# Two pairs of heads in one stretch of attention matmuls, in an attention and SwiGLU kernel on Trainium2

## The chip, the cores and the metric

The kernel runs on one core of one Trainium2 chip. The metric is device time in microseconds (us) of one execution; lower is better. The core's engines are TensorE (PE in the profile; PEld is its weight load), VectorE (DVE), ScalarE (ACT), GpSimd (POOL) and SyncE (SP, which here only issues transfers). They run side by side, each through its own list of instructions in order, and wait for each other by semaphores. Matmuls write PSUM, which has eight banks; everything else lies in SBUF or in device memory.

## The reference

```python
def rmsnorm(x, g):
    return x / np.sqrt(np.mean(x * x, axis=-1, keepdims=True) + 1e-06) * g
q_n, k_n = rmsnorm(q, g_q), rmsnorm(k, g_k)        # q, k, v: (8, 12, 448, 64), float32
scores = np.matmul(q_n, k_n.transpose(0, 1, 3, 2)) / np.sqrt(64)
attn = np.exp(scores - scores.max(-1, keepdims=True))
attn = attn / (attn.sum(-1, keepdims=True) + 1e-09)
x = np.matmul(attn, v)                             # -> rows of (8 * 448, 12 * 64)
xn = rmsnorm(x, rms_g)                             # over 768 columns
g = xn @ w_gate                                    # 768 x 1536
out = (g / (1 + np.exp(-g)) * (xn @ w_val)) @ w_out
```

There are eight sequences of 448 tokens with 12 heads of 64, then a feed-forward net (FFN) over all 3584 tokens, all in float32.

## The kernel before, in words

**Attention** goes by pairs of heads, two heads side by side on the 128 partitions: pairs 0 to 47, six to a sequence, so pair g is place g mod 6 of sequence g // 6. Scores are made transposed, in seven parts of 64 keys by 448 queries a head. `step(g, i)` does three things: the two score matmuls of part i of pair g into a bank of the scores pool (`ps_s`, four banks, tag "s"), the two matmuls of part i of the pair before (`weighted(g - 1, i)`: values by exponentials, into the tile `av`), and the exponentials of the new scores on ACT into a tile `e` (11 buffers). Each of these matmuls uses a quarter of the array, 64 by 64, and the four of a step run side by side. So one call of seven steps makes the scores of pair g and the weighted values of pair g - 1. I call such a run of attention matmuls between FFN matmuls an **excursion**.

The softmax's denominators are made off TensorE: `later_sums(g, n)` has POOL add the seven `e` tiles of a pair into `es` (six adds, lines 904 and 909). At every even pair, `totals(g - 1)` sums two pairs' `es` over the keys with a few small matmuls into `den` (scores pool), ACT copies them, DVE inverts them, and `weigh` multiplies: x = av * rd. ACT then squares x, and POOL adds the squares to `ss`, for the norm ahead of the FFN. After an odd pair the kernel only puts `av` aside (`hold`, one ACT copy), and weighs it at the next `totals`. `av` lies in `ps_m`, a pool of one bank, which the transposes of q and k (tile `tr`) use too.

**The FFN** of a sequence is worked off while the next sequence's attention runs. For the first sequence it is plain matmuls. From the second on, gate and value are 4 groups of 15 products in a scheme with fewer multiplications (`three`; a **product** is four matmuls with 128x128 weights and 224 columns, line 1419), and the out projection has 7 products, or two levels of 7 (`out_quads`, line 1778). Sums of blocks are made by DVE (lines 989, 1610, 1638 and others). The weights are converted once from float64 by DVE, ACT and POOL, while the first sequence's FFN runs; sums of weight blocks are made by DVE during the second (`derive`, lines 1311 to 1346) and third (`derive_q`, lines 1377 to 1380), written to device memory (`kept`, `kept_o`, `kept_q`), and read again by SP into a ring of slots (`w`) for each sequence. A slot is asked for again when TensorE has used it.

**The order** is written out by hand. `pe(fn)` emits a piece of TensorE's work and counts one step; `after(n, fn)` emits something n steps later; `light(fn)` puts small DVE work on a list that is emitted between FFN items. The main loop goes over the pairs. The turn of pair g (places 1 to 5) is: its excursion, then a third of the turn's FFN items (`fill`), the norms and squares of the pairs ahead, the transposes of q and then k of pair g + 1 with another `fill` between them, and a last `fill`. So between two excursions lies the FFN work of one turn, and excursions and FFN alternate from pair 8 to the end. A `fill(hold=True)` leaves one weight conversion of its last item to be emitted within the next excursion.

Until its weights are all made the FFN also depends on the place of an excursion: `derive_q` is tried once within each excursion, and within `fill` only more than four steps after the last excursion's end (`st["block"]`).

`yard` is one SBUF tile in which places for q, k, v, their norms and other small things are cut out by hand (`spot`).

Of the kernel before, what the change touches and what calls it, by code (L numbers as in the profile page):

```python
# [335 lines left out]
def safe_scores(  # L336
# [42 lines left out]
    def after(n, fn):  # L379
        due.append((now["t"] + n, fn))  # L380
# [41 lines left out]
    AT_QK = PER_B  # L422
    AT_V = AT_QK + 3 * PAIR
    AT_OTHER = AT_V + 3 * THIRD
    AT_RS = AT_V
    AT_V1 = AT_RS + 7 * NB
    yard = slots.tile([128, AT_OTHER + PER_B], F32, name="yard")

    def spot(at, n):
        return yard[:, at:at + n]  # L430

    def turned(g):

        return g >= TURNED * NPAIR
# [30 lines left out]
    def squares_turned(g):  # L465

        qk, n = st["qk", g], 2 * NB
        ms = st["ms", g] = spot(AT_RS, 2 * n).rearrange("p (a n) -> p a n", a=2)
        rs = st["rs", g] = spot(AT_RS + (4 + g % 2) * NB + g % 2 * NB // 2, NB + NB // 2)
        def reduce(i, sq):  # L470
            nc.vector.tensor_reduce(out=ms[:, 0, i * NB:(i + 1) * NB], in_=blocks(sq), axis=AX_X, op=ALU.add)
            if i == 1:
                after(1, other)
                after(2, total)
                after(2, root)

        for i in range(2):
            sq = new_sq()
            nc.scalar.activation(sq, qk[:, i], ACT.Square)
            light(lambda i=i, sq=sq: reduce(i, sq))  # L480
        every, first, second = slice(0, NB), slice(NB, NB + NB // 2), slice(NB + NB // 2, n)
        both = slice(0, NB + NB // 2)

        def other():
            for at in (0, 64):
                nc.scalar.copy(ms[at:at + 32, 1, both], ms[at + 32:at + 64, 0, both])
                for to, of in ((every, every), (first, second)):
                    nc.scalar.copy(ms[at + 32:at + 64, 1, to], ms[at:at + 32, 0, of])
# [326 lines left out]
    def weighted(g, i):  # L815

        b, hp = divmod(g, NPAIR)
        if i == 0:
            st["av", g] = ps_m.tile([128, 512], F32, name="av", tag="m")
        for j in range(2):  # L820
            r = across(j)
            vt = st["v", g][r, i] if turned(g) else st["vr", b][r, hp] if i == PARTS - 1 else st["v", g][r, i // NK, i % NK]
            nc.tensor.matmul(st["av", g][own(j), 0:S], lhsT=vt, rhs=st["e", g, i][r], start=i == 0, stop=i == PARTS - 1,  # L823
                             skip_group_check=True)

    def step(g, i):
# [2 lines left out]
        weighted(g - 1, i)  # L829
        if ps is not None:  # L830
            exps(g, i, ps)

    AT_ALIKE = AT_OTHER
    AT_FEW = AT_ALIKE + 128

    def late(g):

# [24 lines left out]
    def totals_folded(g):  # L862

        which = (g - 1, g)
        den = ps_s.tile([128, 512], F32, name="den", tag="s")[:, 0:2 * NB]
        for j in range(2):
            nc.tensor.matmul(den[own(j)], lhsT=alike()[across(j), own(j)], rhs=some_few(0, 2)[across(j)], start=True, stop=True)
        few = some_few(2, 2)
        nc.vector.reciprocal(few, den)
        for i in which:  # L870
            rd = st["rd", i] = tmp.tile([128, S], F32, name="rd", tag="rd", bufs=2)
            nc.vector.transpose(out=blocks(rd), in_=few[:, i % 2 * NB:(i % 2 + 1) * NB].unsqueeze(2).to_broadcast([128, NB, 32]))
            if i < g:
                weigh(i, 3, 4)

    def totals(g):

        if folded(g):
            totals_folded(g)
            return  # L880
        which = (g, g - 1) if g > NPAIR + 1 else (g,)
        den = {i: ps_s.tile([128, 512], F32, name="den", tag="s") for i in which[::-1]}
        for i in which:
            es = st.pop(("es", i))
            for j in range(2):
                to = j if i == g else 1 - j
                nc.tensor.matmul(den[i][own(to), 0:S], lhsT=ones[across(j)], rhs=es[across(j)], start=True, stop=True)
        for i in which[::-1]:
            rd = st["rd", i] = tmp.tile([128, S], F32, name="rd", tag="rd", bufs=2)
            if i == g:  # L890
                nc.scalar.copy(rd, den[i][:, 0:S])
            else:
                for j in range(2):
                    nc.scalar.copy(rd[own(j)], den[i][across(j), 0:S])
        for i in which[::-1]:
            invert(st["rd", i], st["rd", i])
            if i < g:
                weigh(i, 3, 4)

    def later_sums(g, n):  # L900

        def first():
            st["es", g] = tmp.tile([128, S], F32, name="es", tag="es", bufs=2)
            nc.gpsimd.tensor_tensor(st["es", g], st["e", g, 0], st["e", g, 1], ALU.add)  # L904
            more(2)

        def more(*parts):
            for i in parts:
                nc.gpsimd.tensor_tensor(st["es", g], st["es", g], st["e", g, i], ALU.add)  # L909

        after(n, first)
        after(n + 2, lambda: more(3, 4))
        after(n + 3, lambda: more(5, 6))
        if folded(g):
            after(n + 8, lambda: light(lambda: fold(g)))

# [1143 lines left out]
            convert()  # L2060


    at_once(squares(0, 0))
    warm(15)
    reduce, root, scale = norm_rests(0, 0, 2)
# [16 lines left out]
    for g in range(NG + 1):  # L2082
# [51 lines left out]
        if g == NPAIR + 1:  # L2134
# [8 lines left out]
            later_sums(g, 2)  # L2143
            begin(0, 15)
        else:
            hurry_light()
            sums_due = g % 2 == 0
            pe(lambda: (totals(g - 1) if sums_due else None, step(g, 0)))
            if st.pop("held", None):
                convert()  # L2150
            pe(lambda: [step(g, i) for i in (1, 2)])
            derive_q()
            pe(lambda: [step(g, i) for i in (3, 4)])
            pe(lambda: ([step(g, i) for i in (5, 6)], weigh(g - 1, 2) if sums_due else hold(g - 1)))
            if g < NG:
                later_sums(g, 11 if g == 3 * NPAIR else 2)
        st["block"] = now["t"]
        for n in (1, 2):
            if turned(g + n) == (n == 1):
                after(2, lambda g=g + n: load_v(g))  # L2160
        if hp:
            fill()
            norm_k(g + 1, 0)
            if not turned(g + 2):
# [74 lines left out]
```

## Time and profile before

| | |
|---|---|
| median of 3 runs | 1476.36 us (1475.61 to 1476.56) |
| the profiled execution's own time | 1474.93 us |
| its span in the profile | 1473.1 us |
| PE busy | 1453.9 us, 99% |
| DVE, ACT, POOL busy | 1073.0, 620.1, 763.9 us |
| granted TensorE clock | 1.00 |
| excursions between FFN matmuls, pairs 8 to 48 | 41 |

The profile's views used here are the page (busy times), the timeline (instructions in order of time, equal ones merged: start, duration, engine, line, operation, tiles, parts of the array, shape, count, and in brackets the idle time before with what ended it), the waits (engine, line and what was waited for: total us, number, longest), and windows (a stretch of time: its length, then busy us of each engine, the granted clock, the mean share of the DMA engines and GB/s). The trace has two records for each of the program's matmuls, so a product has 8 records. A matmul's duration is longer than the distance to the next one's start, since they are pipelined; distances of starts tell the pace.

### The profile page before, as it was taken

The numbers are of one execution on the slowest core, as the hardware profiler recorded it, in microseconds if no ns is written. First come the engines' busy times: TensorE is split into PE (matmuls) and PEld (weight loads), VectorE is DVE, ScalarE is ACT, GpSimd is POOL, SyncE is SP. The second block draws the span as 40 slices with busy tenths as digits, with TensorE's granted clock in tenths as the row PEclk, the third lists the DMA queues.
The fourth block names the chain that finished last, engine by engine and source line by source line (L and its number), as shares of the span: only waits on it lengthen the run. The fifth ranks groups of instructions, "written<-read, shape, count | busy, mean of one in ns | idle before, by whom it ended". The sixth has DMA issues, their size and how long they took to land.

```text
span 1473.1 us, 25744 instructions
## 1 busy us (share of the span) xinstructions
PE 1453.9 (99%) x8538; PEld 1142.2 (78%) x8538; DVE 1073.0 (73%) x1868; ACT 620.1 (42%) x1551; POOL 763.9 (52%) x684
## 2 busy tenths in 40 slices
PE   9999999999999999999999999999999999999998
PEld 4344445678855788887888889859898799899998
DVE  6788999799975677874579855755679755784665
ACT  7856776455423444234442443444542533101110
POOL 6867997647343363462545744655645842120003
PEclk9999999999999999999999999999999999999999
DMA  8758676776787999777656866677467855597576
GB/s 218 225 158 250 185 240 184 216 252 226 260 267 225 307 314 319 241 248 207 154 165 199 263 191 184 184 227 203 131 191 222 274 171 149 162 305 237 169 231 203
DMA packets 340577, 322.52 MB, mean 219 GB/s; under 512 B 126932, under 2 KB 282068, under 8 KB 340436
## 3 DMA queue, kind: packets, MB, share of 16 engines
q1 hardware_dynamic: 339428, 320.48, 72.9%
q8 instruction: 71, 1.16, 0.3%
q14 instruction: 70, 0.57, 0.1%
q10 hardware_dynamic: 880, 0.30, 0.1%
q0 software_dynamic: 128, 0.00, 0.0%
HBM read 266.90 MB, written 53.77 MB: 218 GB/s over the span
## 4 chain that ended last, share of the span: by engine, by line


## 5 line engine op out<-in xcount | busy, mean ns | idle before, releaser
L909 POOL TENSOR_TENSOR es<-es,e 128x448 f32<-128x448 f32 x205 | 254.5, 1241 | 13.6
L1419 PE MATMUL ff<-x,w 128*128 128x224 f32 x1296 | 258.1, 353 | 0.3 <-DVE pc L1440 0.3
L1419 PEld LDWEIGHTS ff<-x,w 128*128 128x128 f32 x1296 | 243.6, 190 | 3.5 <-issue 2.1
L805 PE MATMUL sc<-qT,kT 64*64 64x448 f32 x1176 | 231.5, 539 | 0.6 <-DVE x L959 0.5
L823 PE MATMUL av<-e,yard 64*64 64x448 f32 x1148 | 224.3, 538 | 0.0
L1419 PE MATMUL ff<-xs,w 128*128 128x224 f32 x832 | 164.5, 353 | 2.7 <-DMA w<-kept 1.9
L1419 PEld LDWEIGHTS ff<-xs,w 128*128 128x128 f32 x832 | 156.3, 190 | 6.2 <-issue 2.1
L805 PEld LDWEIGHTS sc<-qT,kT 64*64 64x64 f32 x1176 | 78.8, 133 | 87.2 <-issue 53.8
L786 POOL TENSOR_TENSOR ss<-ss,rd 128x448 f32<-128x448 f32 x40 | 47.7, 1192 | 157.8 <-ACT rd L785 156.4
L1778 PE MATMUL ff<-w,l 128*128 128x192 f32 x630 | 116.7, 328 | 2.8 <-DVE l L1638 2.2
L1440 DVE TENSOR_TENSOR pc<-ff,l 128x448 f32<-128x448 f32 x56 | 34.8, 622 | 108.7 <-PE ff L1419 85.8
L1869 PE MATMUL ff<-x,w 128*128 128x448 f32 x288 | 111.8, 541 | 0.0
L1778 PEld LDWEIGHTS ff<-w,l 128*128 128x128 f32 x630 | 103.8, 190 | 7.8 <-DVE l L1638 3.0
L823 PEld LDWEIGHTS av<-e,yard 64*64 64x64 f32 x1148 | 77.1, 133 | 36.9 <-issue 36.7
L904 POOL TENSOR_TENSOR es<-e 128x448 f32<-128x448 f32 x41 | 49.1, 1196 | 107.9 <-ACT e L813 79.4
L813 ACT ACTIVATE e<-sc 128x448 f32<-128x448 f32 x168 | 87.9, 548 | 36.7 <-PE sc L805 27.2
L1869 PEld LDWEIGHTS ff<-x,w 128*128 128x128 f32 x288 | 53.3, 190 | 51.1 <-issue 48.2
L811 ACT ACTIVATE e<-sc,yard 128x448 f32<-128x448 f32 x126 | 78.3, 635 | 31.8 <-PE sc L805 23.3
L1419 PE MATMUL ff<-top_x,w 128*128 128x224 f32 x440 | 91.1, 357 | 0.0
L1419 PEld LDWEIGHTS ff<-top_x,w 128*128 128x128 f32 x440 | 81.8, 190 | 11.5 <-issue 8.5
L1437 DVE TENSOR_TENSOR pb<-ff,pb 128x448 f32<-128x448 f32 x84 | 52.2, 622 | 48.9 <-PE ff L1419 48.8
L1736 POOL TENSOR_TENSOR y<-y,pa 128x384 f32<-128x384 f32 x10 | 11.1, 1128 | 144.8 <-DVE y L1844 137.2
(251 smaller groups left out, 2972.6 us busy)
## 6 DMA issues: line engine op xcount, KB each, us to landing
w<-kept SPq DMA_DIRECT2D x380, 256.0 KB, 3.9
w<-kept_q SPq DMA_DIRECT2D x350, 192.0 KB, 3.7
w<-kept_o SPq DMA_DIRECT2D x150, 192.0 KB, 4.0
kept_q<-w SPq DMA_DIRECT2D x63, 192.0 KB, 4.0
raw<-in_moe_w_gate_dram SPq DMA_DIRECT2D x24, 384.0 KB, 4.6
raw<-in_moe_w_val_dram SPq DMA_DIRECT2D x24, 384.0 KB, 4.2
kept<-w SPq DMA_DIRECT2D x48, 192.0 KB, 4.2
raw<-in_moe_w_out_dram SPq DMA_DIRECT2D x24, 384.0 KB, 3.7
```

The source lines that it names most:

```text
L786: after(m, lambda: (nc.gpsimd.tensor_tensor(ss, ss, rd, ALU.add), st.update({("summed", b): hp})))
L805: nc.tensor.matmul(ps[r, 0:S], lhsT=keys(g, r, i), rhs=st["qT", g][r, :], start=True, stop=True)
L811: nc.scalar.activation(e, ps[:, 0:S], ACT.Exp, scale=st["rs", g][:, NB + i:NB + i + 1])
L813: nc.scalar.activation(e, ps[:, 0:S], ACT.Exp)
L823: nc.tensor.matmul(st["av", g][own(j), 0:S], lhsT=vt, rhs=st["e", g, i][r], start=i == 0, stop=i == PARTS - 1, skip_group_check=True)
L904: nc.gpsimd.tensor_tensor(st["es", g], st["e", g, 0], st["e", g, 1], ALU.add)
L909: nc.gpsimd.tensor_tensor(st["es", g], st["es", g], st["e", g, i], ALU.add)
L1419: nc.tensor.matmul(bank[:, w * HT:(w + 1) * HT], lhsT=data(key)[:, (2 * w + c) * 128:(2 * w + c + 1) * 128], rhs=a[left][:, c, :], start=o ...
L1437: nc.vector.tensor_tensor(T[name], ps[:, 0:S], T[name], ALU.add)
L1440: nc.vector.tensor_tensor(T[name], ps[:, 0:S], T[other], what)
L1778: nc.tensor.matmul(ps, lhsT=a[:, j, :], rhs=data(key)[:, n % 2 * HW:(n % 2 + 1) * HW], start=start and j == 0, stop=j == KG - 1, skip_grou ...
L1869: nc.tensor.matmul(bank[w][:, 0:S], lhsT=data(key)[:, c * 128:(c + 1) * 128], rhs=st["x", 0][:, 3 * half + c, :], start=half == c == 0, st ...
```

## The change

Of each sequence, the third and fourth pair (places 2 and 3) and the fifth and sixth (places 4 and 5) are now done in one excursion, from pair 8 on: `leads(g)` is true for pairs 8, 10, 14, 16, 20, 22, 26, 28, 32, 34, 38, 40, 44 and 46, and these 14 are moved from the head of their turn to its end, behind the turn's last `fill`, and so directly ahead of the excursion of the next pair. What goes with it:

- The weighted values of a leading pair are made in the second half of the double excursion, while `av` of the pair before still waits in `ps_m`'s one bank to be weighed. So they go to a bank of the scores pool, which has three left for scores meanwhile.
- POOL's sums of a leading pair's exponentials are emitted within the excursion, one step closer together (`gap`).
- The squares of the two pairs weighed in it are emitted behind the whole excursion (8 and 9, and 7 steps on, in place of 3 and 4, and 2).
- `rs` gets three places in `yard` in place of two, in another part of it.
- Transposes of q and k of both pairs now come ahead of the excursion, and one dead time after an excursion serves for two pairs (`attended`).

```diff
-    AT_RS = AT_V
-    AT_V1 = AT_RS + 7 * NB
+    AT_V1 = AT_V + 7 * NB
+    AT_ALIKE = AT_OTHER
+    AT_FEW = AT_ALIKE + 128
+    AT_RS = AT_FEW + 6 * NB
...
-        rs = st["rs", g] = spot(AT_RS + (4 + g % 2) * NB + g % 2 * NB // 2, NB + NB // 2)
+        rs = st["rs", g] = spot(AT_RS + 4 * NB + g % 3 * (NB + NB // 2), NB + NB // 2)
...
         if i == 0:
-            st["av", g] = ps_m.tile([128, 512], F32, name="av", tag="m")
+            st["av", g] = (ps_s if leads(g) else ps_m).tile([128, 512], F32, name="av", tag="s" if leads(g) else "m")
...
             if i < g:
-                weigh(i, 3, 4)
+                weigh(i, *((8, 9) if leads(g + 1) else (3, 4)))
+
+    def leads(g):
+
+        return g > NPAIR + 1 and g < NG and g % NPAIR in (2, 4)
...
+        gap = 1 if leads(g) else 2
         after(n, first)
-        after(n + 2, lambda: more(3, 4))
-        after(n + 3, lambda: more(5, 6))
+        after(n + gap, lambda: more(3, 4))
+        after(n + gap + 1, lambda: more(5, 6))
...
+    def attend(g):
+
+        hurry_light()
+        sums_due = g % 2 == 0
+        if leads(g):
+            later_sums(g, 2)
+        pe(lambda: (totals(g - 1) if sums_due else None, step(g, 0)))
+        if st.pop("held", None):
+            convert()
+        pe(lambda: [step(g, i) for i in (1, 2)])
+        derive_q()
+        pe(lambda: [step(g, i) for i in (3, 4)])
+        pe(lambda: ([step(g, i) for i in (5, 6)], weigh(g - 1, 7 if leads(g) else 2) if sums_due else hold(g - 1)))
+        if g < NG and not leads(g):
+            later_sums(g, 11 if g == 3 * NPAIR else 2)
+
+    def attended(g):
+
+        for n in (1, 2):
+            if turned(g + n) == (n == 1):
+                after(2, lambda g=g + n: load_v(g))
+        st["block"] = now["t"]
...
         else:
+            if not leads(g):
+                attend(g)
+        if not leads(g):
+            attended(g)
+        if hp:
             hurry_light()
-            sums_due = g % 2 == 0
-            pe(lambda: (totals(g - 1) if sums_due else None, step(g, 0)))
...
             turn_for(g + 1, 1)
-            fill(hold=g % 2 == 1)
+            fill(hold=leads(g) or g % 2 == 1 and not leads(g + 1))
+            if leads(g):
+                attend(g)
+                attended(g)
             continue
```

TensorE at pairs 22 and 23, in the fourth sequence. Before, the last steps of pair 22's excursion are followed by FFN products (`ff`) and the transposes of pair 23 (the numbers of the tiles `qT`, `kT` and `av` tell the pair):

```order
L805 MATMUL sc_4807<-qT_4588,kT_4589 64x448 x2
L823 MATMUL av_4770<-e_4515,yard_111 64x448 x2
L805 MATMUL sc_4814<-qT_4588,kT_4589 64x448 x2
L823 MATMUL av_4770<-e_4522,yard_111 64x448 x2
L1419 MATMUL ff_4706<-xs_4398,w_119 128x224 x4
L1419 MATMUL ff_4718<-top_x_2650,w_119 128x224 x4
L1419 MATMUL ff_4727<-top_x_2651,w_119 128x224 x4
L1419 MATMUL ff_4706<-x_2565,w_119 128x224 x4
L1419 MATMUL ff_4718<-l2_4429,w_119 128x224 x4
L684 MATMUL tr_4888<-ident_130,qn_4610 128x128 x3
```

Now, at the same place:

```order
L807 MATMUL sc_5059<-qT_4619,kT_4620 64x448 x2
L825 MATMUL av_5014<-e_4544,yard_111 64x448 x2
L807 MATMUL sc_5066<-qT_4619,kT_4620 64x448 x2
L825 MATMUL av_5014<-e_4551,yard_111 64x448 x2
L807 MATMUL sc_5079<-qT_4828,kT_4829 64x448 x2
L825 MATMUL av_5082<-e_5017,yard_111 64x448 x2
L807 MATMUL sc_5087<-qT_4828,kT_4829 64x448 x2
L825 MATMUL av_5082<-e_5028,yard_111 64x448 x2
```

The scores go on with the next pair's q and k, and the values with a new `av`; no FFN matmul stands between.

POOL around the second half of the fourth sequence's out projection, before. `es` are sums of exponentials (those of pair 32, from `es<-e` on), `ss` the squares, `pb`, `pc`, `y` and `pa` sums for the out projection, `yard` the norms of pair 34:

```order
L1736 TENSOR_TENSOR pb<-pb,pa 128x384 x2
L1736 TENSOR_TENSOR pc<-pc,pb 128x384 x2
L492 TENSOR_TENSOR yard<-yard 128x21
L493 TENSOR_SCALAR yard<-yard 128x21
L496 TENSOR_TENSOR yard<-yard,mhalf 128x21
L497 TENSOR_TENSOR yard<-yard 128x448
L904 TENSOR_TENSOR es<-e 128x448
L909 TENSOR_TENSOR es<-es,e 128x448
L1736 TENSOR_TENSOR y<-y,pc 128x384 x2
L786 TENSOR_TENSOR ss<-ss,rd 128x448
L909 TENSOR_TENSOR es<-es,e 128x448 x4
L1736 TENSOR_TENSOR pc<-pc,pa 128x384 x2
```

Now:

```order
L1740 TENSOR_TENSOR pb<-pb,pa 128x384 x2
L1740 TENSOR_TENSOR pc<-pc,pb 128x384 x2
L494 TENSOR_TENSOR yard<-yard 128x21
L495 TENSOR_SCALAR yard<-yard 128x21
L498 TENSOR_TENSOR yard<-yard,mhalf 128x21
L499 TENSOR_TENSOR yard<-yard 128x448
L1740 TENSOR_TENSOR y<-y,pc 128x384 x2
L1740 TENSOR_TENSOR pc<-pc,pa 128x384 x2
L1740 TENSOR_TENSOR pa<-pa,pb 128x384 x2
```

The six sums of pair 32 have left the out projection; they now stand behind it, in the double excursion.

DVE at the end of the second sequence's out projection, just behind pair 20's excursion, before: `y<-ff` are the out projection's last additions, `xs<-x`, `top_x<-x,xs` and `l<-x,top_x` block sums for the third sequence's products, and four rows of `w<-w` are one job of `derive_q`.

```order
L1665 TENSOR_TENSOR y<-ff,pb 128x384
L989 TENSOR_TENSOR xs<-x 128x448 x2
L1665 TENSOR_TENSOR y<-ff,pc 128x384
L989 TENSOR_TENSOR top_x<-x,xs 128x448 x2
L1665 TENSOR_TENSOR y<-ff,pc 128x384
L989 TENSOR_TENSOR l_4429<-x,top_x 128x448
L1377 TENSOR_TENSOR w<-w 128x192
L1378 TENSOR_TENSOR w<-w 128x192
L1379 TENSOR_TENSOR w<-w 128x192
L1380 TENSOR_TENSOR w<-w 128x192
```

Now, with pair 20's excursion still to come, further jobs stand among these additions, of which this is one:

```order
L1669 TENSOR_TENSOR y<-ff,pc 128x384
L993 TENSOR_TENSOR xs<-x 128x448
L1381 TENSOR_TENSOR w<-w 128x192
L1382 TENSOR_TENSOR w<-w 128x192
L1383 TENSOR_TENSOR w<-w 128x192
L1384 TENSOR_TENSOR w<-w 128x192
L993 TENSOR_TENSOR xs<-x 128x448
L631 TENSOR_REDUCE ms<-sq 128x6 x2
L1669 TENSOR_TENSOR y<-ff,pb 128x384
```

In the whole order nine of the 21 jobs now stand ahead of the first DVE addition of the third sequence's products (line 1440, now 1444), where six stood before.

More of the change, by code (lines that the diff above doesn't have):

```diff
@@ L831, in step @@
             exps(g, i, ps)
-    AT_ALIKE = AT_OTHER
-    AT_FEW = AT_ALIKE + 128
     def late(g):
@@ L897, in totals @@
             if i < g:
-                weigh(i, 3, 4)
+                weigh(i, *((8, 9) if leads(g + 1) else (3, 4)))
+    def leads(g):
+        return g > NPAIR + 1 and g < NG and g % NPAIR in (2, 4)
     def later_sums(g, n):
@@ L2145, in safe_scores @@
         else:
-            hurry_light()
-            sums_due = g % 2 == 0
-            pe(lambda: (totals(g - 1) if sums_due else None, step(g, 0)))
[L2149 to L2161, printed above, removed]
+            if not leads(g):
[3 more added lines that the diff above has]
+        if hp:
+            hurry_light()
             fill()
```

## The prediction

> **What bounds the kernel now.** I read the page's busy times first, then what TensorE waits for, then the timeline around one excursion, then windows of the stages that have waits.
>
> ```profile
> span 1473.1 us, 25744 instructions
> PE 1453.9 (99%) x8538; PEld 1142.2 (78%) x8538; DVE 1073.0 (73%) x1868; ACT 620.1 (42%) x1551; POOL 763.9 (52%) x684
> PEclk9999999999999999999999999999999999999999
> ...
> PE ff L1778 <- DVE l L1638: 2.2, 2, 1.2
> PE ff L1419 <- DMA w<-kept: 1.9, 2, 1.0
> PE ff L1419 <- DVE pb L1437: 1.6, 3, 1.1
> ```
>
> TensorE is busy for 99% of the span at full clock, so the end is set by TensorE's own list, and a change counts only if it shortens that list's pace or one of its few waits. No matmul is removed here. What can be won is in the pace, and that is in the starts around one excursion, pair 21's:
>
> ```profile
> 539.26 1.75 PE L1419 MATMUL ff<-xs,w 128*128 128x224 f32 x8 [0.97 <-DMA w<-kept]
> 540.94 0.59 PE L805 MATMUL sc<-qT,kT 64*64 64x448 f32 x2
> 541.37 0.54 PE L805 MATMUL sc<-qT,kT 64*64 64x448 f32 x2
> 541.75 0.54 PE L805 MATMUL sc<-qT,kT 64*64 64x448 f32 x2
> ...
> 545.88 0.54 PE L805 MATMUL sc<-qT,kT 64*64 64x448 f32 x2
> 546.37 3.29 PE L1419 MATMUL ff<-top_x,w 128*128 128x224 f32 x16
> ...
> 515.33 3.19 PE L1419 MATMUL ff<-top_x,w 128*128 128x224 f32 x16
> ```
>
> Sixteen records that follow FFN work take 3.19 us, so one start follows another by (3.19 - 0.35) / 15 = 0.19 us. Within the excursion starts go by (545.88 - 541.37) / 12 = 0.376 us, four matmuls in each such slot. Four places are slower. Into the excursion: the last FFN record starts at 539.26 + 1.75 - 0.35 = 540.66, the first score at 540.94, 0.28 later, 0.09 too many. Its first slot lasts 0.43, 0.05 too many. Out of it: 546.37 - 545.88 = 0.49, 0.11 too many. And the first 16 FFN records take 3.29, 0.10 too many. One excursion therefore costs **0.35 to 0.36 us** beside its matmuls.
>
> **The change, part by part.**
>
> *Joined excursions.* Fourteen pairs lose their own way in and out; a double excursion pays once. The joint itself should keep the pace of 0.376: the next q and k are turned ahead of it. Gain: 14 x 0.356 = **5.0 us**.
>
> *A bank less for scores.* In the second half of a double excursion, three banks take the scores. ACT's list in pair 22's excursion, at the end:
>
> ```profile
> 510.13 2.00 ACT L813 ACTIVATE e<-sc 128x448 f32<-128x448 f32 x4
> 512.39 1.24 ACT L813 ACTIVATE e<-sc 128x448 f32<-128x448 f32 x2 [0.27 <-PE sc L805]
> 513.90 0.54 ACT L813 ACTIVATE e<-sc 128x448 f32<-128x448 f32 x1 [0.27 <-PE sc L805]
> ```
>
> Four exponentials together take 2.00, 0.5 each, and from the fifth on ACT waits for scores. A step takes two slots, 0.75. With three banks a bank must be read 2.25 after its scores began; scores 0.75, a delay of some 0.3 and an exponential of 0.54 make 1.6. Spare: 0.65 us. I take 0; if ACT came later by one more instruction of 0.54 there would still be no wait, by two it would be 0.4 for each double excursion, 6 us in all. `av` waits for an exponential that is likewise three back.
>
> The Trainium skill, TensorEngine Tiling (Array Packing), Performance Considerations, warns against this: tiles of the array speed up the matmuls, not the emptying of PSUM, which may become the bottleneck. By that rule the second half would go at ACT's pace; the rows above show ACT waiting for TensorE, so the sum stands.
>
> *Sums of exponentials.* `es` of a leading pair moves from the FFN that followed it into the excursion: six adds of 1.24. An `e` buffer is needed again eleven parts on, so the second pair's fifth part waits for the first pair's first add. Both parts of that add are there after the second step of fourteen; the buffer is needed at the twelfth, some nine steps or 6.8 us later, for 1.2 of work. POOL may be about 5 us late without harm. In the FFN the adds cost something:
>
> ```profile
> 642.35 0.55 DVE L1638 TENSOR_TENSOR raw<-raw 128x384 f32<-128x384 f32 x1
> 647.73 5.47 POOL L909 TENSOR_TENSOR es<-es,e 128x448 f32<-128x448 f32 x4
> 652.14 1.48 DVE L1638 TENSOR_TENSOR raw<-raw 128x384 f32<-128x384 f32 x1
> 651.04 2.47 PE L1778 MATMUL ff<-w,l 128*128 128x192 f32 x12 [0.51 <-DVE pa L1827]
> 653.67 2.22 PE L1778 MATMUL ff<-w,raw 128*128 128x192 f32 x12 [0.16 <-DVE raw L1638]
> ...
> 648.41 2.11 PE L1778 MATMUL ff<-w,raw 128*128 128x192 f32 x12
> 829.32 2.11 PE L1778 MATMUL ff<-w,raw 128*128 128x192 f32 x12
> 831.46 2.22 PE L1778 MATMUL ff<-w,l 128*128 128x192 f32 x12
> 833.81 2.22 PE L1778 MATMUL ff<-w,raw 128*128 128x192 f32 x12
> 835.86 1.14 PE L1778 MATMUL ff<-w,l 128*128 128x192 f32 x6
> ```
>
> The same DVE addition takes 0.55 alone and 1.48 while POOL adds, and TensorE waits for DVE just there. Twelve records should go by in 12 x (2.11 - 0.33) / 11 = 1.95 us. From 648.41 to 651.04 and on to 653.67 it is 2.63 twice, 1.4 too many; from 829.32 to 835.86, three runs, 6.54, 0.7 too many. These are the out projections around pairs 26 and 32; the third of this kind, around pair 44, I take like the second: 2.8 in all. The order shows the adds gone from there. I take half, **1.4**, between 0 and 2.8, since pair 26's, 32's and 44's own excursion, a rest for DVE in the middle of that work, goes too.
>
> *DVE's list in the second sequence's products.* Here excursions gave DVE time to catch up:
>
> ```profile
> 297.00:412.50 115.50, 113.03 (x709) 92.09 (x708) 107.36 (x164) 57.60 (x202) 64.06 (x55) 1.00 0.76 247
> 325.00:331.20 6.20, 6.20 (x65) 2.31 (x64) 6.03 (x13) 4.54 (x9) 0.00 (x0) 1.00 0.77 241
> 353.40:358.80 5.40, 5.40 (x57) 2.04 (x56) 5.23 (x8) 3.27 (x6) 2.84 (x3) 1.00 0.83 245
> 507.50:513.70 6.20, 6.20 (x65) 2.32 (x64) 3.82 (x8) 5.07 (x10) 0.00 (x0) 1.00 1.02 336
> 402.62 1.78 PE L1419 MATMUL ff<-raw,w 128*128 128x224 f32 x8 [1.12 <-DVE pb L1437]
> ```
>
> DVE (the third busy time of a row) is at 107.4 of 115.5, and inside the excursions of pairs 16 and 17 at 11.3 of 11.6, of which some 3.8 belong to the attention, as pair 22's shows; 7.5 us were work left over from the FFN. With twice as much FFN in a row the left-over grows until TensorE waits for a bank, and in the double excursion DVE may run dry. Bounds: -2.5 (the 115.5 - 113.0 that TensorE now idles here are gone) to +7.5 (below). Two double excursions touch the stage (pairs 14 and 15, 16 and 17), and their leading pairs' adds no longer slow DVE between them. I take **+1.0**.
>
> *Weights in the third sequence's products.* The DMA engines are full here, and the excursions were their rest:
>
> ```profile
> 412.50:470.00 57.50, 57.50 (x272) 31.72 (x272) 34.91 (x62) 18.64 (x45) 24.61 (x23) 1.00 0.80 238
> 480.90:507.50 26.60, 25.61 (x139) 24.58 (x135) 19.20 (x43) 9.16 (x22) 11.40 (x13) 1.00 0.97 308
> 513.70:540.90 27.20, 25.89 (x139) 24.56 (x135) 21.30 (x42) 9.66 (x23) 15.39 (x15) 1.00 0.97 299
> 505.86 1.75 PE L1419 MATMUL ff<-xs,w 128*128 128x224 f32 x8 [0.97 <-DMA w<-kept]
> kept_q<-w SPq DMA_DIRECT2D x63, 192.0 KB, 4.0
> kept_q<-w SPq DMA_DIRECT2D x21, 96.0 KB, 4.2
> ```
>
> Each stretch of 16 or 17 products ends with a load that is 1 us late, and now 32 products come in a row between pairs 21 and 22: up to 6.2 us, pair 22's excursion, of loading that is not covered. Against it, the order has nine jobs of `derive_q` ahead of these products in place of six. A job reads two blocks of 192 KB and stores 63 / 21 = 3 of 192 and one of 96, 1056 KB; three are 3.2 MB, 10 us at 308 GB/s, moved to a stage whose DMA share is 0.80, with 57.5 x 0.2 = 11.5 us free. That is more than the 6.2. I take 0 between -2 (both waits gone) and +6.2.
>
> Sum: -5.0 - 1.4 + 1.0 = **-5.4 us**. The profiled execution took 1474.93 (1.8 beside its span) and would take 1469.5; the median of the runs shown is 1476.36, and from it I predict **1471.0 us**.
>
> **Rivals.**
>
> *DVE runs dry (slower).* If each of the two double excursions in the second sequence's products holds only its own 3.8 of work for DVE, 2 x (11.6 - 3.8) = 15.6 us of DVE time are lost, 8.1 were idle before, and 7.5 us must be made up with TensorE waiting: 1476.36 - 5.0 + 7.5 = 1478.9. It turns slower beyond (8.1 + 5.0) / 2 = 6.5 us idle in each. For it: 11.3 of 11.6 before. Against it: block sums emitted ahead of the excursion can still be waiting in DVE's list. Chance 0.09.
>
> *The loads take the gain back (no change).* If the jobs moved ahead don't relieve the stream, pair 22's missing rest costs up to 6.2; less the 1.4, 1476.4 - 5.0 - 1.4 + 6.2 = 1476.2. For it: 0.97 of DMA share. Against it: the 10 us above. Chance 0.22.
>
> *The waits go too.* If the late loads (2 us), DVE's waits at the second sequence's products (2.5) and all of the 2.8 vanish, 1476.4 - 5.0 - 7.3 = 1464.1; with half of them, 1467.7. For it: work moved ahead, adds moved out of the way. Against it: DVE at 107.4 of 115.5. Chance 0.08.
>
> *The joint costs what an excursion did.* If TensorE paused at the change of pair as at the way in and out, nothing of the 5.0 is won. Against it: steps within an excursion change tiles just so without a pause. Within the no-change case.
>
> **How the numbers follow.** The forecast has 0.61, with 1469.0 to 1473.3 as its own range. About 0.2%, 3 us, is what a measurement here tells from no change. Faster by more: 0.61 + 0.08 less a little at the edge = 0.67; within: 0.24; slower: 0.09. The range for 8 in 10 leaves out the slower case and half of the better one: 1467.5 to 1476.5.
>
> **What would show it.** Starts at a joint 0.376 apart, and 27 ways in and out in place of 41; the DVE additions in the out projections of pairs 26, 32 and 44 at 0.55, and TensorE without waits there; the wait for `w<-kept` not longer than 2 us in all. Wrong would be: TensorE waiting for ACT within double excursions, a DVE share well under 0.9 in the stage of the second sequence's products with longer waits for `pb` and `pc`, or late loads ahead of pair 22.

## The result, and the profile after

The changed kernel takes **1495.2 us** (median; 1493.7 to 1497.3) where the kernel before takes 1476.0: 1.0132 of the time, with a 95% interval from 1.0117 to 1.0148. It is 19.2 us slower; 5.4 less were forecast, and the range ended at 1476.5. The page of the changed kernel, and what TensorE waits for:

```profile
span 1491.9 us, 25757 instructions
PE 1454.2 (97%) x8538; PEld 1150.0 (77%) x8538; DVE 1077.7 (72%) x1868; ACT 619.6 (42%) x1551; POOL 763.3 (51%) x684
...
PEclk9999999989999999999999999999999999999999
```

```profile
PE ff L1423 <- DVE pb L1441: 7.3, 6, 2.2
PE ff L1423 <- DVE w L1318: 6.8, 2, 3.8
PE ff L1423 <- DMA w<-kept: 5.9, 5, 1.6
PE ff L1697 <- DMA w<-kept_o: 2.7, 4, 1.2
```

TensorE's busy time is what it was (1454.2 against 1453.9), and 18.5 us more of the span are idle. That the busy times agree is chance: in the windows below it is 4.2 more from pair 13 to pair 18, where some matmuls ran at a lower clock, and 4.2 less from pair 24 on. (Lines have moved: 1419 is now 1423, 1437 is 1441, 1778 is 1782, 805 is 807, 813 is 815.) The wait for `w` of line 1318 is new: these are `derive`'s sums of weight blocks in the second sequence. Those for `w<-kept` and `pb` were 1.9 and 1.6, that for `kept_o`, weights of the second sequence's out projection, did not exist.

Where the time went is read from windows (length, busy us of PE, PEld, DVE, ACT and POOL, clock, DMA share, GB/s). The cuts are the same places of the program in both: the starts of pair 13's, 18's and 24's excursions, and the end. First the kernel before, then the changed one:

```profile
244.30:379.90 135.60, 133.74 (x804) 102.76 (x803) 120.53 (x176) 70.27 (x251) 81.65 (x75) 1.00 0.75 238
...
571.60:1473.10 901.50, 891.30 (x5542) 786.18 (x5541) 612.23 (x1086) 306.16 (x679) 401.50 (x339) 1.00 0.70 207
```

```profile
244.90:393.40 148.50, 137.94 (x807) 106.76 (x806) 119.36 (x179) 69.99 (x251) 80.46 (x75) 0.95 0.67 219
...
595.60:1491.90 896.30, 887.06 (x5542) 791.02 (x5541) 606.57 (x1086) 305.79 (x679) 403.10 (x339) 1.00 0.70 204
```

From pair 13 to pair 18, the second sequence's products, 148.5 in place of 135.6: **12.9 lost**, at a clock of 0.95. From pair 18 to pair 24, that sequence's out projection and the third's products, 202.2 in place of 191.7: **10.6 lost**, by the unrounded starts. From pair 24 to the end **5.3 won**, and before pair 13 0.6 lost. DVE does the same work in the first window, 119.4 us against 120.5: it isn't busier, it is later.

The first loss is made at three products. Two stand behind the double excursion of pairs 14 and 15, one behind that of pairs 16 and 17. TensorE, VectorE and SyncE's queue there:

```profile
303.12 3.29 PE L1423 MATMUL ff<-x,w 128*128 128x224 f32 x16
306.25 1.68 PE L1423 MATMUL ff<-x,raw 128*128 128x224 f32 x8
310.94 2.79 PE L1423 MATMUL ff<-x,w 128*128 128x224 f32 x8 [3.02 <-DVE w L1318]
317.49 3.35 PE L1423 MATMUL ff<-raw,w 128*128 128x224 f32 x8 [3.77 <-DVE w L1318]
...
382.09 2.33 PE L1423 MATMUL ff<-raw 128*128 128x224 f32 x8 [2.23 <-DVE pb L1441]
```

```profile
304.93 0.62 DVE L1441 TENSOR_TENSOR pa<-ff,pa 128x448 f32<-128x448 f32 x1 [5.74 <-PE ff L1423]
...
307.96 0.63 DVE L1441 TENSOR_TENSOR pb<-ff,pb 128x448 f32<-128x448 f32 x1 [0.89 <-PE ff L1423]
308.50 0.76 DVE L1315 TENSOR_TENSOR w<-w,raw 128x512 f32<-128x512 f32 x1
309.29 1.50 DVE L1318 TENSOR_TENSOR w<-w,raw 128x512 f32<-128x512 f32 x1
313.76 1.16 DVE L1441 TENSOR_TENSOR pc<-ff,pc 128x448 f32<-128x448 f32 x2 [2.97 <-PE ff L1423]
...
316.75 0.69 DVE L1318 TENSOR_TENSOR w<-w,raw 128x512 f32<-128x512 f32 x1
...
370.38 0.62 DVE L1441 TENSOR_TENSOR pb<-ff,pb 128x448 f32<-128x448 f32 x1 [2.85 <-PE ff L1423]
```

```profile
289.30 1.37 SPq L1294 DMA_DIRECT2D w<-kept  x3
...
297.45 6.36 SPq L550 DMA_DIRECT2D yard<-in_v_dram  x4
303.86 0.58 SPq L1294 DMA_DIRECT2D raw<-kept  x1
```

Three things can be read, and each is a theory. The sum that the product at 310.94 needs (308.50 and 309.29) is the last thing VectorE does before it: **the order puts the sum directly ahead of its product**. VectorE was idle for 5.74 us in the double excursion: **it ran dry** (the first rival of the prediction). And SyncE's queue stood for 6.36 us at the loads of `v`, which wait for the end of the double excursion, with a raw weight block (`raw<-kept`) behind them: **the queue was blocked**. A fourth thing is that the 8 records of a product take 2.79 and 3.35 behind these waits, not 1.68. The granted clock is half in that stretch (the 0.50 below):

```profile
311.52:321.76 10.24, 6.47 (x20) 5.32 (x19) 4.48 (x8) 0.02 (x1) 1.74 (x5) 0.50 0.24 77
```

The third wait, at 382.09, is for a bank that VectorE empties late. VectorE had rested 2.85 us up to 370.38, at the end of the second double excursion; from 373.41 to the wait's end it worked without a rest.

What can be counted in the order: at how many steps behind its sum, or behind the request for its load, a product stands.

| | before | changed |
|---|---|---|
| sums of the second sequence, first nine | 3 2 3 4 6 10 8 9 9 | 5 6 6 8 10 14 14 **0 0** |
| next nine | 6 7 7 8 13 13 12 13 13 | 4 6 2 3 4 4 4 5 5 |
| out projection's weights, last load of each of the last six half products | 4 5 7 3 5 6 | 4 **1** 3 2 4 2 |
| third sequence's weights, the 14th to the last of the 32 products that now lie between pairs 21 and 22 | 3 to 10, mostly 7 and more | 3 to 6 |

Nothing about these sums stands in the diff. Rules that count steps place them: a load is asked for only when 7 places of the ring are free (5 after nine sums), a sum is made only 5 steps behind the request for its blocks, and not in an excursion or the two steps behind it. With pair 14's excursion no longer ahead of these products, the first sums are made sooner and hold places, and the last raw block of the group is asked for behind the eighth of its products in place of the first. Then the double excursion passes, in which no sum is made, and the two sums that need that block come directly ahead of their products.

### The profile page after: what moved, and what is told of

It is laid out like the page before. It is cut to its first block, busy times and chain, and to the rows that moved or that the text cites. A ratio compares the mean times of both kernels' runs of the same rounds, so it can differ in the third digit from the quotient of the medians.

```text
span 1491.9 us, 25757 instructions
## 1 busy us (share of the span) xinstructions
PE 1454.2 (97%) x8538; PEld 1150.0 (77%) x8538; DVE 1077.7 (72%) x1868; ACT 619.6 (42%) x1551; POOL 763.3 (51%) x684
## 4 chain that ended last, share of the span: by engine, by line
## 5 line engine op out<-in xcount | busy, mean ns | idle before, releaser
L813 ACT ACTIVATE e<-sc,yard 128x448 f32<-128x448 f32 x126 | 77.9, 635 | 20.6 <-PE sc L807 10.6
```

The costliest lines, as they stand in the source:

```text
L813: nc.scalar.activation(e, ps[:, 0:S], ACT.Exp, scale=st["rs", g][:, NB + i:NB + i + 1])
```

## Experiments

**1. Which joints lose.** `leads` alone is altered.

```diff
-        return g > NPAIR + 1 and g < NG and g % NPAIR in (2, 4)
+        return g > 4 * NPAIR and g < NG and g % NPAIR in (2, 4)   # late_only: pairs 26 and on
+        return g in (14, 16)                                      # second_only
+        return g in (20, 22)                                      # third_only
```

> Only the eight leading pairs from 26 on (fourth sequence and later) are joined; pairs 8 to 22 go as before. From the start of pair 24's excursion to the end the changed kernel took 896.3 us (1491.9 - 595.65) where the kernel before took 901.6 (1473.1 - 571.55). Theory that the loss lies only in the second and third sequence: the time is that of before less 5.3, 1470.7 of 1476.0. Rival that each joint costs something wherever it stands: the 19.2 us of loss over 14 joints are 1.37 each, eight of them make +11, 1487.

> Only pairs 14 and 16 are joined with the pairs behind them (the excursions among the second sequence's products). From the start of pair 13's excursion to that of pair 18's the changed kernel took 148.49 us, the kernel before 135.64. Theory that each stage loses by itself: +12.9, 1488.9 of 1476.0. Rival that the second sequence's lateness is passed on and makes the third's too: another 10.6 on top, 1499.

> Only pairs 20 and 22 are joined with the pairs behind them. From the start of pair 18's excursion to that of pair 24's the changed kernel took 202.27 us, the kernel before 191.63. Theory that each stage loses by itself: +10.6, 1486.6 of 1476.0. Rival that the third sequence only suffers from what the second was late with: the two joints alone remain, -0.7, 1475.3.

| joined pairs | median, us | ratio to before (1475.9), 95% interval | expected |
|---|---|---|---|
| 26 and on | 1470.3 | 0.9965 (0.9953 to 0.9978) | 1470.7 |
| 14, 16 | 1488.6 | 1.0090 (1.0075 to 1.0106) | 1488.9 |
| 20, 22 | 1487.1 | 1.0076 (1.0060 to 1.0091) | 1486.6 |

The parts add up: -5.6 + 12.7 + 11.2 = +18.3, of 19.2; most of the rest is the 0.6 from before pair 13. A joint does not cost of itself, and the third sequence's loss doesn't come down from the second's. The eight late joints alone are faster than either kernel.

**2. The second sequence's sums.** One number of the changed kernel is altered, so that the same two sums stand 18 steps ahead of their products. The excursions stay where they are.

```diff
-                kind, keep_free = "wg1", 4 if asked["derived"] >= len(RIGHT_G) else 6
+                kind, keep_free = "wg1", 4
```

> The changed kernel with one number altered: a load of a raw weight block in the second sequence asks for 5 free places in the ring from the start, not for 7 until the first nine sums are made. The excursions stand where they stand in the changed kernel; the sums for the first group's last two products stand 18 steps ahead of them in the order in place of 0. Theory that the waits at 310.9 and 317.5 come from where the order puts those two sums: they go, 3.0 and 3.8 us, and so does the half pace behind them (8 records in 2.79 and 3.35 where 1.68 is usual, and transposes, some 3.3 us): 1495.2 - 10.1 = 1485.1. Rival that VectorE runs dry in the double excursions (5.7 us idle in the first) and must make up for that whatever the order: as much waiting at other places, 1494 to 1496. Rival that the loads of v, which stand in SyncE's queue until the double excursion ends, hold the weights back: these loads are not moved, 1494 to 1496.

Measured: 1488.1 us, 1.0083 (1.0067 to 1.0098), 7 less than the changed kernel. The windows from pair 13 to pair 18 and from pair 18 to pair 24, then VectorE and the same two products behind the first double excursion, and SyncE's queue:

```profile
245.40:381.60 136.20, 133.35 (x806) 102.70 (x805) 115.10 (x171) 70.17 (x251) 81.30 (x74) 1.00 0.70 227
...
381.60:593.50 211.90, 193.51 (x1066) 141.26 (x1066) 150.22 (x265) 73.56 (x186) 81.84 (x76) 0.98 0.87 274
```

```profile
305.88 0.62 DVE L1441 TENSOR_TENSOR pa<-ff,pa 128x448 f32<-128x448 f32 x1 [5.74 <-PE ff L1423]
...
308.71 1.68 PE L1423 MATMUL ff<-x,w 128*128 128x224 f32 x8
310.22 1.68 PE L1423 MATMUL ff<-raw,w 128*128 128x224 f32 x8
...
300.07 5.52 SPq L550 DMA_DIRECT2D yard<-in_v_dram  x4
```

VectorE is idle for the same 5.74 us, the queue stands at `v` for 5.52, and yet neither product waits: the stage takes 136.2 in place of 148.5. So the two long waits came from **the place of the sums in the order**. This run alone does not clear the queue, since the raw blocks of these sums are now asked for earlier too; the changed kernel's trace does. From the end of the product before (307.96 and 313.76) to the end of each sum VectorE has no rest, so a block that landed sooner would not have made the sum sooner. And in the order these blocks are asked for ahead of the loads of `v` (the last at 289.30); the one that stands behind them belongs to the next group.

For the third wait the two theories about VectorE are not told apart: here it is gone, but VectorE's rest at the end of the second double excursion is gone as well (0.15 us in place of 2.85).

The total did not come down by the 10.1 expected. The next stage, from pair 18 to pair 24, takes 211.9 where the changed kernel took 202.2, so most of what was won is lost there. (The profiled execution took 1491.2 us, 3.1 above the median.) With another rule of asking, other loads come late: one of the out projection's, asked for 4 steps ahead in the changed kernel, now stands 2 steps ahead.

```profile
PE ff L1697 <- DMA w<-kept_o: 6.2, 4, 2.8
```

That is 6.2 of waiting in place of 2.7. Two waits for VectorE that the changed kernel doesn't have, 1.8 and 1.1 us, and a clock of 0.98 are most of the rest. So it is not excluded that VectorE must make up some time elsewhere; but that did not make these two products wait.

**3. The third sequence's weights.** Pairs 20 and 22 alone are joined. In the first run a load may be asked for with one free place fewer, which moves each request one product ahead and leaves the jobs of `derive_q` where they are. In the second these jobs stand back while fewer than 7 blocks are asked for ahead of the product (the second piece notes how far the products are).

```diff
-            kind, keep_free = "wg" if key[0] == "wg" else "w", 3
+            kind, keep_free = "wg" if key[0] == "wg" else "w", 2 if key[1] == 2 and key[0] == "wg" else 3
```

```diff
+        if st.get("taken", 0) > next_gate[0] and asked["n"] - st["taken"] < 7:
+            return False
         if not todo_q or sums_o or now["t"] - asked.get("at_q", 0) < ...
...
+            if key in uses:
+                st["taken"] = uses.index(key) + 1
             pe(fn)
```

> Pairs 20 and 22 joined as in the run that joins these two alone (1487.1 us, 11.2 over the kernel before), and one number altered: a load of a weight block for the third sequence's products asks for 3 free places in the ring, not 4. The jobs of derive_q stand at the same places and move the same bytes; in the order a weight block is now asked for one product earlier, 4 to 7 steps ahead of its use between pairs 21 and 24 where it was 3 to 6 and, in the kernel before, 7 to 10. Theory that the weights are late because the order asks for them too late (from issue to landing a load takes 4 to 5.5 us here, three products of 1.51 are 4.5): the waits for w<-kept in these products, 6.7 us, and the half pace behind the longest, 1.7, go for the most part, and the time is 1479 to 1481; the waits in the out projection (some 3) and for pb stay. Rival that the DMA engines are too full for this stretch without the excursions' rest: the same bytes in the same stretch, 1486 to 1488.

> Pairs 20 and 22 joined alone, and derive_q stands back while fewer than 7 weight blocks are asked for ahead of the product: 10 jobs become 5 between pairs 21 and 22, the rest come later; a block is asked for 5 to 8 steps ahead of its use. Theory of the late asking: the waits for w<-kept go, 6.7 and 1.7 of half pace, and with fewer jobs on VectorE some of the waits for pb (4.5) too: 1487.1 - 8.4 - 2 = 1477, with 1.5 on either side; the out projection's waits, some 3, stay. Rival of the full DMA engines: here the bytes are spread too, so it also expects 1477 to 1480; the run that leaves the jobs where they are tells the two apart. If neither, 1487.

Measured: 1482.3 (1.0047, 1.0032 to 1.0063) and 1479.9 (1.0034, 1.0021 to 1.0047), beside 1474.9 of the kernel before, where the two joints without either edit had 1.0076. TensorE's waits in these products, for the joints alone, with earlier requests, and with jobs that stand back:

```profile
PE ff L1423 <- DMA w<-kept: 6.3, 4, 2.6
PE ff L1423 <- DVE pb L1441: 2.9, 2, 1.5
```

```profile
PE ff L1423 <- DVE pb L1441: 2.9, 2, 1.6
PE ff L1423 <- DMA w<-kept: 1.3, 3, 0.5
```

```profile
PE ff L1425 <- DVE pb L1443: 1.6, 2, 1.4
PE ff L1425 <- DMA w<-kept: 1.2, 1, 1.2
```

With the jobs at the same places, so the same bytes in the same stretch, and one step more of lead, 5 of 6.3 us of waiting for weights are gone: they were **asked for too late**, not held up by full DMA engines. All the loads that came late in the changed kernel and with these two joints alone stand 3 or 4 steps ahead of their products, none 5 or more; not every load with 3 or 4 was late. (In the kernel before these products had 3 to 10 steps, not 7 to 10 as the expectation has it.) The time fell by 4.3 us (0.0029 of it) and not by the 7 expected; some of the rest is the out projection's, whose waits for `w<-kept_o` are 3.3 us here and 2.2 for the joints alone.

The jobs that stand back also take 1.3 off the waits for `pb` in this stretch, VectorE's part; 0.8 of it comes back behind pair 24.

**4. The sums of exponentials in the out projections.** The kernel before, with no pair joined; POOL's adds of three pairs come 7 steps later.

```diff
-                later_sums(g, 11 if g == 3 * NPAIR else 2)
+                later_sums(g, 11 if g == 3 * NPAIR else 9 if g in (26, 32, 44) else 2)
```

> The kernel before, no pair joined; only the sums of exponentials of pairs 26, 32 and 44 are emitted 7 steps later, behind the out projection's second half. Theory that GpSimd's additions there slow VectorE's and make TensorE wait (1.4 around pair 26, 0.7 around 32, 0.7 around 44): the waits at 651, 654, 831, 834, 1160 and 1162 go, the VectorE additions between take 0.55 to 0.7, and the time is 1476.0 - 2.8 = 1473.2. Rival that the waits come from these pairs' own excursions in the middle of the out projection: they stay, 1476.

Measured: 1472.6 against 1474.9, 0.9984 (0.9975 to 0.9993), so -2.4 us (-3.7 to -1.0). The place of pair 26, first the changed kernel, then this one:

```profile
666.15 2.11 PE L1782 MATMUL ff<-w,raw 128*128 128x192 f32 x12
668.10 2.11 PE L1782 MATMUL ff<-w,l 128*128 128x192 f32 x12
670.05 2.11 PE L1782 MATMUL ff<-w,raw 128*128 128x192 f32 x12
...
666.95 0.55 DVE L1642 TENSOR_TENSOR l<-l,raw 128x384 f32<-128x384 f32 x1
```

```profile
649.10 2.11 PE L1778 MATMUL ff<-w,raw 128*128 128x192 f32 x12
651.05 2.11 PE L1778 MATMUL ff<-w,l 128*128 128x192 f32 x12
653.00 2.11 PE L1778 MATMUL ff<-w,raw 128*128 128x192 f32 x12
...
650.70 0.54 DVE L1638 TENSOR_TENSOR l<-l,raw 128x384 f32<-128x384 f32 x1
```

Three runs of 12 records follow each other by 1.95, and VectorE's addition takes 0.54 where it took 1.48 beside POOL's adds. The excursion's place has no part in it: here it is where it was. The Trainium skill, GPSIMD Engine Reference, 1. Specifications, says that GpSimd and VectorE share their SBUF interfaces, with contention in VectorE's instructions that have two SBUF inputs. These additions have two; the 0.54 and 1.48 agree.

**5. The price of a wait.** A kernel of its own, run once: streams of matmuls of a product's shape, and a wait for VectorE between two of them, 60 waits of ten lengths. It leaves out all of the reference's work.

> A kernel for the price of a wait alone; it computes nothing of the reference, and fills the output's rows with a constant. TensorE runs streams of 32 to 37 matmuls (128x128 weights, 224 columns, the shape of a product), and between two of them waits for a chain of VectorE additions of 0 to 10 times some 0.5 us, six times each length. In the changed kernel TensorE went at half pace (starts 0.373 us apart, not 0.188) for about 3.4 us after waits of 2.4, 3.2 and 4.2 us, and not after waits of 1.7 and less. Theory that it hangs on the length of the wait with a fixed limit near 2 us: all streams behind waits over 2.4 us start so, none behind 1.7 and less. Rival that it is a matter of where the wait falls in a window of about 3.4 us that runs by itself: behind waits of 2 to 5 us some streams are slowed and some not, all behind longer ones, and a slowed stretch is 3.4 us long. Rival that the half pace had another cause: none is slowed.

The start of this kernel's TensorE timeline; a stream of 64 records takes 12.4 us when nothing slows it:

```profile
20.58 12.38 PE L51 MATMUL ff<-x,w_next 128*128 128x224 f32 x64 [0.98 <-DVE w_next L64]
37.35 13.92 PE L51 MATMUL ff<-x,w_next 128*128 128x224 f32 x64 [4.40 <-DVE w_next L64]
53.70 14.06 PE L51 MATMUL ff<-x,w_next 128*128 128x224 f32 x64 [2.43 <-DVE w_next L64]
...
90.20 12.37 PE L51 MATMUL ff<-x,w_next 128*128 128x224 f32 x64 [1.76 <-DVE w_next L64]
...
236.94 12.75 PE L51 MATMUL ff<-x,w_next 128*128 128x224 f32 x66 [2.42 <-DVE w_next L64]
```

Behind waits of 0.98 and 1.76 none of 12 streams is slowed; behind 2.4 and 3.1 us 8 of 12 are, by 1.4 to 1.7 us (two rows above show both, after 2.43 and 2.42 us; 12.75 is what a stream of 66 takes when nothing slows it); behind 3.7 and more all 36, by 1.4 to 3.0. In a slowed stretch starts are 0.373 apart, not 0.189. Where it starts within a stream it lasts 3.3 to 3.4 us; where the stream itself starts slow, 2.8 to 6.1. So it isn't a fixed limit of length but where the wait falls, the second theory, except that the stretch may be longer.

The traces also keep the times at which the granted clock changed, and these settle where. They lie on a grid of 3.41 us in each of the twelve traces here. I took TensorE's idle share in each piece of the grid from its matmul records, whose ends are modelled. Of the pieces at full clock, all 52 with 0.57 or more idle were followed by half clock, and none of the 4922 with 0.54 or less. From half clock it went back to full behind all 52 pieces with 0.15 or less idle, and stayed at half behind all 33 with 0.20 or more. Some 0.55 of 3.41 is 1.9 us, so by this estimate a shorter wait alone never halves the clock, one over 3.8 always does, as it fills that share of one of two pieces, and between them the place decides.

**6. All pairs joined with altered rules, and the best set of joints.** The first run has all 14 pairs joined, experiment 2's number, and other distances between `derive_q`'s jobs (99 keeps all but the first of them back until the third sequence's weights are asked for). The second joins pairs 8 and 10 and all from 26 on.

```diff
-... now["t"] - asked.get("at_q", 0) < (4 if asked["n"] <= next_gate[0] else 3) ...
+... now["t"] - asked.get("at_q", 0) < (99 if asked["n"] <= next_gate[0] else 4) ...
```

> All 14 pairs joined as in the change, with both rules altered: loads of raw weight blocks in the second sequence ask for 5 free places from the start, and the jobs of derive_q keep a distance of 4 steps in place of 3, all but the first only from the third sequence's products on. In the order the sums of the second sequence stand 5 to 18 steps ahead of their products, the out projection's weights are asked for 4 to 8 steps ahead but for one load with 2, the third sequence's 3 to 8 steps. Theory that the loss is late asking alone: 1476 - 5.0 (joints) - 2.5 (waits in the later out projections) + 4.5 for the one load with a lead of 2 (2.9 and half pace, as in the run with one number altered) + 3 for waits for pb: 1476, between 1473 and 1479. Rival that the double excursions cost of themselves in these two sequences, in VectorE's idle time or in transfers that pile up: no better than the run with one number altered, 1486 to 1490.

> Pairs 8 and 10 and all from 26 on joined, the second and third sequence's as before: the change without the four joints that lose. Account of the parts: 0.71 are won at pairs 8 and 10, 0.33 of it lost to a wait within the second of these excursions (177.5), so 0.4 better than the eight joints alone: 0.9962 of the time before, 1470. Rival that a joint in the first sequence loses as in the second (weights are converted there): over 0.9975, 1472 and more.

Measured: 1485.5 (1481.4 to 1487.7), 1.0078 (1.0063 to 1.0094); and 1471.0, 0.9970 (0.9958 to 0.9982). The second lies between its theory, 0.9962, and its rival, 0.9975, and its interval holds both; nor can it be told from the eight late joints alone (0.9965). The first missed: 1476 was expected. In its profiled execution, of 1481.4 us, the second sequence's products take 136.5, near the 135.6 of the kernel before, and the stage from pair 18 to pair 24 takes 196.9, 5.2 more than before; but the jobs that were put off now come in the fourth sequence, whose out projection waits for what they make (`kept_q`) and for weights:

```profile
650.36 2.19 PE L1782 MATMUL ff<-w,raw 128*128 128x192 f32 x12 [0.50 <-DMA w<-kept_q]
...
660.45 1.75 PE L1423 MATMUL ff<-xs,w 128*128 128x224 f32 x8 [1.86 <-DMA w<-kept]
```

From pair 24 to the end this kernel needs 901.1 (1479.3 - 578.2), as the kernel before: the late gain of 5.3 is gone. Lateness was moved on, not taken away. The other three executions take 4 to 6 us more. They left no trace, but their granted clock is on record: 0.996, 0.996 and 0.997, where the profiled one has 0.999. A loss of 0.002 to 0.003 of 1485 us is 3 to 4.5 us at most, so slowed stretches can be the larger part; which waits brought them is not known.

## Why the prediction was wrong, step by step

**What bounds the kernel** was read rightly: TensorE's list and its few waits. So was the price of an excursion, as far as the sum below shows it.

**Joined excursions, -5.0: right.** Scores around the joint of pairs 22 and 23, and ACT beside it:

```profile
562.54 0.54 PE L807 MATMUL sc<-qT,kT 64*64 64x448 f32 x2
...
562.92 0.54 PE L807 MATMUL sc<-qT,kT 64*64 64x448 f32 x2
...
563.29 0.54 PE L807 MATMUL sc<-qT,kT 64*64 64x448 f32 x2
...
565.77 0.54 ACT L815 ACTIVATE e<-sc 128x448 f32<-128x448 f32 x1 [0.21 <-PE sc L807]
```

Starts are 0.37 to 0.38 apart across the joint, there are 27 ways in and out, and of the 5.3 won from pair 24 on, 8 x 0.356 = 2.85 are put down to this. That is a difference, not a measurement of the joints alone: the other 2.45 belong to the sums of exponentials, which experiment 4 measured by themselves.

**A bank less, 0: right** from pair 14 on: ACT still waits 0.2 for each score. In the excursion of pairs 10 and 11 one score starts 0.35 late, as it waits for ACT to copy `den`, which lies in the same pool; the term had left `den` out. In experiment 2's trace the same wait is 1.40.

**Sums of exponentials, -1.4: right in kind, too small.** The rest of the 5.3 is 2.45, and experiment 4 measured 2.4 (1.0 to 3.7): near the upper bound of 2.8. Half was taken because the pair's own excursion had to go too; that excursion had no part in it.

**VectorE's list in the second sequence's products, +1.0, at most 7.5: here the prediction failed.** It cost 12.9 + 0.7 = 13.6 (0.7 is what two joints win). The step priced how much VectorE has to do and how long it rests, and took the sums' places in the order as they were. The excursion was also what the rules of asking and summing count steps from; two sums came to stand directly ahead of their products. Their waits of 3.0 and 3.8 us and the half clock behind them are some 10 us. The third wait, 2.2, with the half clock behind it, is some 4. The rival "DVE runs dry" had the sign and even the idle time (5.74 in the first), but not the cause of the two long waits: with the same idle time they are gone. The third wait looks as that rival has it, a rest of 2.85 us and then work that TensorE waits for; whether the rest or the order brought it stays open. That a share of VectorE well under 0.9 would show it wrong did come true (119.4 of 148.5).

**Weights in the third sequence's products, 0, at most 6.2: failed as well.** It cost 10.6 + 0.7 = 11.3. The working weighed bytes, three jobs' 10 us of transfers, and didn't ask when each weight is asked for. In experiment 3 a load takes 3.7 to 5.5 us from issue to landing (4.7 at the median, between 500 and 546 us with pairs 20 and 22 joined), three products 4.5; the late ones were asked for 3 or 4 steps ahead, and one step more took most of the waiting away with the same bytes. The relief was not there either: ten jobs stand among the 32 products between pairs 21 and 22, as five and five did before. The ones that went ahead are missing behind pair 23, where one is left of five. And the jobs ahead, counted as relief, made the out projection's weights late, 2.7 us that no term had. They are late with pairs 20 and 22 joined alone too, and not with 14 and 16; in experiment 6, with these jobs put off, the last six half products have 4 to 6 steps again and only one load, with 2, is late. And 6.2 was no bound: it was one excursion's length, and what came were 4.0 more of waiting for weights (5.9 against 1.9), those 2.7, and 2.9 more of waits for `pb` (4.0 against 1.1).

**Not on the list at all:** that a wait over some 2 us can cost TensorE's pace afterwards. The trace of before has no such wait, so nothing there could show it.

## What to carry to other kernels

Where rules that count steps or free places set an order, moving one piece of work moves what the rules place: count, in the new order, how many steps ahead of its use each load and each sum stands, stage by stage, before pricing anything by throughput. Here a load took up to 5.5 us from issue to landing and a product 1.5, and loads asked for 3 or 4 steps ahead were late where those with one step more mostly were not. And apply such a move only where nothing is being made just in time: the eight late joints win 5.6 us, the four in the stages that make the weights lose 24.

## What the runs showed of the hardware

TensorE's pace after a wait: up to 1.8 us of waiting cost nothing more, 2.4 to 3.1 us cost another 1.4 to 1.7 in two cases of three, 3.7 us and more always cost 1.4 to 3.0; in the changed kernel 2.2 us was enough once. The clock is set anew on a grid of 3.41 us: half, where TensorE idled over some 0.55 of the piece before. Of the changed kernel's clock slices one is an 8; the window's mean shows it better, 0.95 over 148.5 us. The Trainium skill, TensorE: Matmul & The Clock Gate, Part 1: The HAM clock gate, has a clock of half rate after an idle window of some 3.4 us that runs by itself. The half pace, the 3.41 us and the chance by position agree; that 2.4 us of waiting can be enough does not follow from a whole idle window, and here the measurement decides.
